# Products of zeros ahead of the first scores, and squares in pieces of two heads

## The chip, the cores and the metric

One core of a Trainium2 chip runs the kernel. The metric is the device time of one execution in microseconds; the kernel before took 604.68 us (median of 3 runs, 604.56 to 605.29). The core has four engines that matter here: TensorE (PE: matrix products; its weight loads are a row of their own, PEld), VectorE (DVE), ScalarE (ACT) and GpSimd (POOL). SP issues transfers. Each engine takes its instructions strictly from its own queue, in the order in which the program was built; semaphores hold an instruction until what it needs is there.

## The reference

Cosine attention over 8 batches, 12 heads, 448 tokens, 64 columns a head, and then a mixer with a low-rank product over the tokens and a two-layer network (MLP):

```python
q_n = q / (norm(q) + 1e-6);  k_n = k / (norm(k) + 1e-6)
attn = softmax(q_n @ k_n.T / tau)
x = (attn @ v)                       # heads side by side: 448 x 768
u = x + ((x.T @ U) @ V).T            # U: 448 x 32, V: 32 x 448
out = u + relu(u @ w_ch1) @ w_ch2    # 768 -> 3072 -> 768
```

## The kernel before

The work goes batch by batch. **Statistics**: q and k of four heads come in one transfer each (`load_qk`; batch 0's first two heads by SP, the next two by POOL). `squares` squares them on ScalarE or VectorE (L456, L458) and sums each head's 64 columns on VectorE (L462); `scales` makes from this the inverse norm (ScalarE's logarithm and exponential L475, L478, VectorE L481, L483), and `norm` multiplies (L537, tile `xn`, "unit buffer"). A pair of heads is then transposed into `qkT`: for batches 0 and 1 by TensorE (`flip`, L374) with copies out of its bank by ScalarE or VectorE (L827, L829), later by a transposing transfer. **Attention**: for each pair, seven score products of 128x448 (L573), seven exponentials on ScalarE (L578), 32 products with the values (L595, into the ring `av` of two banks), and a reciprocal and a scaling on VectorE (L602, L604) into `X_sb`. **Low rank**: `stage0` makes A = U'X (L652) and then u = X + V'A: products (L631 and L733 in batch 0, L687 after it) and VectorE's sums (L696, L698, L701). **MLP**: up products with w1 (L763), the rectifier on ScalarE or VectorE (L786, L788), down products with w2 (L797), sums into `O_sb` (L806) and out.

The PSUM banks are split into three rings: `mm` (3 banks: transposes, up and down products and others), `sc` (3: scores, and batch 1's low-rank products) and `av` (2).

The order on each engine is written by a planner that is part of the kernel. Every operation is an `Op` with an engine, a guessed duration, what it depends on, and the ring slots that it takes and frees. `Plan.run` plays them in time; an engine that is free takes the first operation that is ready. TensorE's operations stand in streams, tried in the order in which the streams were made: transposes, batch 0's scores, value products, low rank, other scores, MLP. What the planner writes is the order of the instructions; its times are not used for anything else. So an edit of a guessed duration, or one more operation, can move instructions anywhere in the program. For the first pair of batch 0 the guesses are larger than elsewhere: 0.09 for a transpose, 0.31 for a score product, 0.09 for a value product, against 0.05, about 0.19 and 0.033 later.

In this program the ring of squares (`sq`) has two buffers for four heads each.

Of the kernel before, what the change touches and what calls it, by code (L numbers as in the profile page):

```python
# [11 lines left out]
BF = mybir.dt.bfloat16  # L12
# [192 lines left out]
def kernel(  # L205
# [12 lines left out]
    nc = tc.nc  # L218
# [13 lines left out]
    EPS = 1e-6  # L232
    PE_BATCHES = 2
    LATE, VLATE = 8.0, 3.2

    const = ctx.enter_context(tc.tile_pool(name="const", bufs=1))
    pool = ctx.enter_context(tc.tile_pool(name="pool", bufs=1))
# [9 lines left out]
    def ring(n, shape, dt, name, space=None):  # L247
        p = space or pool
        return Ring(n, lambda i: p.tile(shape, dt, name=name, tag=name, bufs=n))
# [7 lines left out]
    v_t = fixed(2, [128, H, 4, D + 2], BF, "v_nat")  # L257

    r_ld, r_xn, r_attn = fixed_ring(ld_t), fixed_ring(xn_t), fixed_ring(attn_t)
    r_sq = ring(2, [SCH, G, SC * D], BF, "sq")  # L260
    r_ss = ring(4, [SCH, 2, G, SC], FP, "ss")
    r_ln = ring(4, [SCH, 2, G, SC], FP, "ln")
    r_inv = ring(4, [SCH, 2, G, SC], FP, "inv")
# [34 lines left out]
    U_sb = const.tile([128, 2, 4, R], BF, name="U_sb")  # L298
    V_sb = const.tile([128, PAD + S + PAD], BF, name="V_sb")
    ident = const.tile([128, 128], BF, name="ident")  # L300
    w1_sb = const.tile([128, CC, F], BF, name="w1_sb")

    nc.scalar.preload_act_table_set("natural_log_exp_and_others")
# [17 lines left out]
    pe_a = plan.stream("PE")  # L321
    pe_sc = plan.stream("PE")
    pe_mlp = plan.stream("PE")
    pool_q = plan.stream("POOL")

    def pe_t(n):
# [115 lines left out]
    def squares(b, g, ld, ops, lo, ii, ss, pr, on, hold, then):  # L442

        red = []
        for i in ii:
            for a0 in range(0, g, G):
                a1 = min(g, a0 + G)
                sq = Slot(r_sq, 1)
                n = 256 * (a1 - a0)
                o = Op(on, {"ACT": act_t(n), "DVE": dve_t(n, 1.45)} if "/" in on else act_t(n) if on == "ACT" else dve_t(n, 1.45), None,  # L450
                       deps=[ops[i], *hold], acq=[sq], prio=pr + 0.2, fast=True)

                def square(o=o, i=i, a0=a0, a1=a1, sq=sq):
                    x, y = ld.tile[:, i, lo + a0:lo + a1, :], sq.tile[:, 0:a1 - a0, :]
                    if o.by == "ACT":
                        nc.scalar.activation(out=y, in_=x, func=AF.Square)  # L456
                    else:
                        nc.vector.tensor_mul(y, x, x)  # L458
                o.fn = square
                plan.add(o)  # L460
                red.append(plan.add(Op("DVE", dve_t(256 * (a1 - a0)),
                    lambda i=i, a0=a0, a1=a1, sq=sq: nc.vector.reduce_sum(  # L462
                        ss.tile[:, i, a0:a1, :].rearrange("p h c -> p (h c)"),
                        sq.tile[:, 0:a1 - a0, :].rearrange("p h (c d) -> p (h c) d", d=D),
                        axis=AX.X),
                    deps=[o, *then], acq=[ss], rel=[sq], prio=pr + 0.1)))
        return red
# [49 lines left out]
    def norm(b, p, ld, la, inv, a, deps, pr):  # L517


        by_pe = b < PE_BATCHES  # L520
        first = b == 0 and p == 0
        xn, qkT = Slot(r_xn, 3 if first else 2 if by_pe else 1), Slot(r_qkT, 7)
        need = [xn_set[count[0] % len(xn_t)]]
        count[0] += 1

        def part(i, h0=0, h1=2):
            def fn():
                n = h1 - h0
                src = ld.tile[:, i, la + h0:la + h1, :].rearrange("p h (c d) -> p h c d", d=D)
                sc = inv.tile[:, i, a + h0:a + h1, :].unsqueeze(3).to_broadcast([SCH, n, SC, D])  # L530
                if i == 0:
                    dst = xn.tile[:, 8:12, :].rearrange("p c (h d) -> p h c d", h=2)
                else:
                    dst = xn.tile.rearrange("p b e -> p (b e)")[:, 0:9 * 128].rearrange(
                        "p (h x) -> p h x", h=2)[:, h0:h1, 0:SC * 128].rearrange(
                        "p h (c e) -> p h c e", c=SC)[:, :, :, 0:D]
                nc.vector.tensor_mul(dst, src, sc)  # L537
            return plan.add(Op("DVE", dve_t(256 * (h1 - h0)), fn, deps=need + [deps[i]], acq=[xn],
                               rel=[getattr(ld, "slot", ld), inv], prio=pr))

        if first:
            ops = [part(0), part(1, 0, 1), part(1, 1, 2)]
            blocks = [(8, 12, ops[0]), (0, 4, ops[1]), (4, 8, ops[2])]
        else:
            ops = [part(1), part(0)]
            blocks = [(0, 8, ops[0]), (8, 12, ops[1])]
        if not by_pe:
            done = [plan.add(Op("SP", 0.1, lambda: nc.sync.dma_start_transpose(
                out=qkT.tile, in_=xn.tile.rearrange("p b e -> p (b e)")), deps=ops, acq=[qkT],
                rel=[xn], prio=0, lat=("x", 0.05 * 84, LATE)))]  # L550
        else:
            done = []
            for b0, b1, o in blocks:
                done.append(flip(
                    pe_tp, [(lambda z=z: xn.tile[:, z, :]) for z in range(b0, b1)], SCH,
                    lambda: qkT.tile, (lambda t_, x, b0=b0, b1=b1: key_tiles(t_, x, b0 // 4, b1 // 4)
                                   if b == 0 and b0 < 8 else [(t_[:, b0:b1, :], x)]),
                    [o], [qkT], [xn], 1, "ACT/DVE", 0.09 if first else 0.05, b == 0 and b0 < 8))
        got[b, p, "qkT"] = (qkT, lambda m: (done[:2] if m < 3 else done) if first else done, done)
        return ops  # L560


    def attention(b, p, X):
        off = PAD * (b % 2)
        qkT, qdeps, _ = got.pop((b, p, "qkT"))
        attn = Slot(r_attn, 2)
        exps = {}
        for m in (0, 1, 2, 6, 3, 4, 5) if b == 0 else range(7):
            sc = Slot(r_sc, 1)

            def score(sc=sc, m=m):
                kT = qkT.tile[:, 0:8, :].rearrange("p b s -> p (b s)")
                nc.tensor.matmul(out=sc.tile[:, 0:S], lhsT=kT[:, 128 * m:128 * (m + 1)],  # L573
                                 rhs=qkT.tile[:, 8:12, :].rearrange("p c s -> p (c s)"),
                                 start=True, stop=True)
            o = plan.add(Op("PE", 0.31 if b == 0 and p == 0 else pe_t(S), score, deps=qdeps(m), acq=[sc], rel=[qkT]),
                         pe_first if b == 0 else pe_sc)
            exps[m] = plan.add(Op("ACT", act_t(S), lambda sc=sc, m=m: nc.scalar.activation(  # L578
                out=attn.tile[:, m, off:off + S], in_=sc.tile[:, 0:S], func=AF.Exp,
                scale=inv_tau), deps=[o], acq=[attn], rel=[sc], prio=0.1 if b == 0 else 1))  # L580
        last_exp[b] = exps[5]
        if b == 0 and p == 0:
            last_exp["first"] = [exps[1]]
        muls = []
        for hh in range(2):
            h = 2 * p + hh
            av, rd = Slot(r_av, 1), Slot(r_rd, 1)
            mine = [3 * hh, 3 * hh + 1, 3 * hh + 2, 6] if b == 0 else [4 * hh, 4 * hh + 1, 4 * hh + 2, 3]
            need = [exps[m] for m in mine]
            for t in range(4):  # L590
                for j in range(4):
                    first, last = t == 0 and j == 0, t == 3 and j == 3
                    def fn(t=t, j=j, h=h, mine=mine, av=av):
                        m = mine[j]
                        nc.tensor.matmul(  # L595
                            out=av.tile[:, t, 0:D + 1],
                            lhsT=attn.tile[:, m, 128 * t:128 * (t + 1)],
                            rhs=v_t[b % 2][:, h, j, 0:D + 1], start=(j == 0), stop=(j == 3))
                    o = plan.add(Op("PE", 0.09 if b == 0 and p == 0 else 0.033, fn,
                        deps=need + got[b, h, "v"] + attn_set + [v_set[b % 2]] if first else (), acq=[av] if first else [],  # L600
                        rel=[attn] if last else []), pe_av)
            r = plan.add(Op("DVE", 0.20, lambda av=av, rd=rd: nc.vector.reciprocal(  # L602
                out=rd.tile, in_=av.tile[:, :, D:D + 1]), deps=[o], acq=[rd], prio=1))
            muls.append(plan.add(Op("DVE", dve_t(256), lambda av=av, rd=rd, h=h: nc.vector.tensor_mul(  # L604
                X.tile[:, :, h * D:(h + 1) * D], av.tile[:, :, 0:D],
                rd.tile.to_broadcast([128, 4, D])), deps=[r],
                acq=[X], rel=[av, rd], prio=1)))
        last_av[b, p] = o
        return muls
# [258 lines left out]
                       in_=V_f().rearrange("r (s c) -> r c s", c=SC))  # L868


    w2_ops = []
    NW = 4
    THIRDS = [(0, 4), (4, 8), (8, 12)]
# [109 lines left out]
```

## Time and profile before

| | |
|---|---|
| median of 3 runs | 604.68 us |
| profiled execution, its own time | 604.68 us |
| its span, first to last instruction | 602.8 us |
| busy: TensorE, weight loads | 586.0 us (97%), 347.7 us |
| busy: VectorE, ScalarE, GpSimd | 295.9, 277.9, 116.3 us |
| mean granted TensorE clock | 0.997 |
| first matmul | at 7.24 us |
| first up product of batch 1 | at 111.14 us |

A line of the timeline gives the start and the length in us, the engine, the source line, the operation, the tile written and the tiles read, the shapes and how many were merged. A line of the groups gives the sum of the busy time and the mean duration in ns. The chain of waits is followed back from the last instruction; each piece says what the end of the program hung on at that time. Matmuls are pipelined: the length of a single one includes its way through the array, and a run of n of them gives their pace. Other groups that the text uses:

```profile
L374 PE MATMUL tp<-ident,xn 112*128 112x112 bf16 x144 | 12.0, 234 | 9.2 <-DVE xn L537 9.1
L604 DVE TENSOR_TENSOR X_sb<-av,rd 128x256 bf16<-128x256 f32 x96 | 40.3, 421 | 1.8
L701 DVE TENSOR_TENSOR u_nat<-mm,X_sb 128x384 bf16<-128x384 f32 x36 | 19.1, 552 | 15.5 <-PE mm L687 15.4
```

### The profile page before, as it was taken

The page shows a single profiled execution, that of the slowest core. Times are in us where ns is not written, and L with a number is a line of the kernel's source. Part 1 is how long each engine was busy: PE and PEld are TensorE (multiplying, and loading weights), DVE is VectorE, ACT ScalarE, POOL GpSimd, SP SyncE. Part 2 cuts the span into 40 slices and gives each one's busy share as a digit, 9 for nine tenths or more (in the row PEclk, how much of TensorE's full clock was granted, in tenths as well). Part 3 has the DMA queues.
Part 4 walks back from the last instruction along what each step waited for, and adds up shares of the span by engine and source line. Part 5 has one row for each costly group of instructions (what it writes and reads, how often), then busy time and mean ns, then how long its engine had stood idle before and what let it go on. Part 6 is the DMA issues. An engine that isn't in the chain of part 4 may idle for free.

```text
span 602.8 us, 11404 instructions
## 1 busy us (share of the span) xinstructions
PE 586.0 (97%) x4702; PEld 347.7 (58%) x4725; DVE 295.9 (49%) x630; ACT 277.9 (46%) x601; POOL 116.3 (19%) x178
## 2 busy tenths in 40 slices
PE   4899999999999999999999999999999999999997
PEld 2566666555565665666445666566545666654565
DVE  8968749989997998554721244014300210110011
ACT  7777762477775277316741067505642025014300
POOL 8155434153613516000600000000000000000000
PEclk9899999999999999999999999999999999999999
DMA  9999999999998989715932132030002110310021
GB/s 147 187 162 119 200 204 119 142 161 112 153 166 138 187 128 150 104 53 93 123 26 66 53 74 47 1 93 27 15 1 53 52 40 1 89 43 1 0 54 53
DMA packets 150164, 54.81 MB, mean 91 GB/s; under 512 B 115040, under 2 KB 150112, under 8 KB 150112
## 3 DMA queue, kind: packets, MB, share of 16 engines
q0 software_dynamic: 72864, 25.73, 38.4%
q1 hardware_dynamic: 77184, 28.32, 25.1%
q8 instruction: 37, 0.61, 0.4%
q14 instruction: 15, 0.12, 0.1%
q10 hardware_dynamic: 64, 0.02, 0.0%
HBM read 52.25 MB, written 11.01 MB: 105 GB/s over the span
## 4 chain that ended last, share of the span: by engine, by line
PE 89%; DVE 7%; ACT 2%; issue 1%; DMA 1%
PE mm L763 35%; PE mm L797 32%; PE sc L573 10%; PE av L595 7%; DVE ss L462 2%; DVE xn L537 2%; PE tp L374 1%; PE mm L687 1%; ACT attn L578 1%; DVE sq L458 1%; DVE u_nat L701 1%; PE mm L652 1%; DVE O_sb L806 1%; PE sc L763 1%; DMA raw_uv<-in_q_dram 1%
## 5 line engine op out<-in xcount | busy, mean ns | idle before, releaser
L763 PE MATMUL mm<-uT,w_sb 128*128 128x384 bf16 (+1 forms) x1112 | 236.4, 353 | 1.5 <-DVE relu L788 0.4
L797 PE MATMUL mm<-w_sb,relu 128*128 128x384 bf16 (+1 forms) x1368 | 233.8, 324 | 0.1
L578 ACT ACTIVATE attn<-sc 128x448 bf16<-128x448 f32 x336 | 165.1, 552 | 111.1 <-PE av L595 56.4
L797 PEld LDWEIGHTS <-relu 128*128 128x128 bf16 x1368 | 132.5, 98 | 85.9 <-issue 0.4
L763 PEld LDWEIGHTS <-w_sb 128*128 128x128 bf16 x1152 | 112.1, 98 | 103.5 <-issue 1.5
L786 ACT ACTIVATE relu<-mm 128x512 bf16<-128x512 f32 (+1 forms) x157 | 85.8, 547 | 130.6 <-PE mm L763 130.1
L806 DVE TENSOR_TENSOR O_sb<-mm,u_nat 128x384 f32<-128x384 f32 (+1 forms) x57 | 31.1, 549 | 213.5 <-PE mm L797 210.0
L573 PE MATMUL sc<-qkT 128*128 128x448 bf16 x336 | 106.6, 364 | 1.8 <-ACT qkT L827 0.6
L595 PEld LDWEIGHTS <-attn 128*128 128x128 bf16 x1536 | 62.5, 99 | 18.2 <-issue 3.0
L418 POOL DMA_DIRECT2D v_nat<-in_v_dram x98 | 63.1, 652 | 32.0 <-DMA w_sb<-in_moe_w_ch_dram 13.1
L595 PE MATMUL av<-v_nat,attn 128*128 128x65 bf16 x1536 | 66.4, 195 | 0.3 <-DVE X_sb L604 0.3
L537 DVE TENSOR_TENSOR xn<-qk_nat,inv 112x512 bf16<-112x512 bf16 x94 | 61.8, 687 | 2.7 <-DMA qkT<-xn 2.6
L462 DVE TENSOR_REDUCE ss<-sq 112x16 f32<-112x1024 bf16 (+1 forms) x50 | 58.0, 1166 | 0.8 <-ACT sq L456 0.4
L396 POOL DMA_DIRECT2D qk_nat<-in_q_dram x24 | 17.2, 717 | 133.8 <-DVE xn L537 100.4
L573 PEld LDWEIGHTS <-qkT 128*128 128x128 bf16 x336 | 29.6, 99 | 20.6 <-issue 5.7
L604 DVE TENSOR_TENSOR X_sb<-av,rd 128x256 bf16<-128x256 f32 x96 | 40.3, 421 | 1.8
L602 DVE RECIPROCAL rd<-av 128x4 f32<-128x4 f32 x96 | 17.1, 179 | 38.6 <-PE av L595 37.9
L458 DVE TENSOR_TENSOR sq<-qk_nat 112x1024 bf16<-112x1024 bf16 x45 | 29.8, 671 | 0.0
L788 DVE TENSOR_SCALAR relu<-mm 128x384 bf16<-128x384 f32 (+1 forms) x32 | 19.7, 615 | 14.6 <-PE mm L763 13.8
L701 DVE TENSOR_TENSOR u_nat<-mm,X_sb 128x384 bf16<-128x384 f32 x36 | 19.1, 552 | 15.5 <-PE mm L687 15.4
L374 PE MATMUL tp<-ident,xn 112*128 112x112 bf16 x144 | 12.0, 234 | 9.2 <-DVE xn L537 9.1
L475 ACT ACTIVATE ln<-ss 112x32 f32<-112x32 f32 (+2 forms) x26 | 6.0, 230 | 28.6 <-DVE ss L462 28.6
(60 smaller groups left out, 169.4 us busy)
## 6 DMA issues: line engine op xcount, KB each, us to landing
qk_nat<-in_q_dram POOLq DMA_DIRECT2D x23, 224.0 KB, 5.4
qk_nat<-in_k_dram POOLq DMA_DIRECT2D x23, 224.0 KB, 6.2
w_sb<-in_moe_w_ch_dram POOLq DMA_DIRECT2D x4, 1152.0 KB, 13.6
w_sb<-in_moe_w_ch_dram POOLq DMA_DIRECT2D x8, 576.0 KB, 15.7
out_dram<-O_sb SPq DMA_DIRECT2D x15, 168.0 KB, 2.3
out_dram<-O_sb SPq DMA_DIRECT2D x16, 144.0 KB, 2.1
out_dram<-O_sb SPq DMA_DIRECT2D x16, 120.0 KB, 2.0
out_dram<-O_sb SPq DMA_DIRECT2D x16, 96.0 KB, 2.2
```

Source lines behind the costliest of these rows:

```text
L418: nc.gpsimd.dma_start(out=vb[p0:p0 + s1 - s0, hs, j, 0:D], in_=v[b, hs].rearrange("h (s c) d -> c s h d", c=SC)[c, s0:s1]),
L458: nc.vector.tensor_mul(y, x, x)
L462: lambda i=i, a0=a0, a1=a1, sq=sq: nc.vector.reduce_sum(ss.tile[:, i, a0:a1, :].rearrange("p h c -> p (h c)"), sq.tile[:, 0:a1 - a0, :].re ...
L537: nc.vector.tensor_mul(dst, src, sc)
L573: nc.tensor.matmul(out=sc.tile[:, 0:S], lhsT=kT[:, 128 * m:128 * (m + 1)], rhs=qkT.tile[:, 8:12, :].rearrange("p c s -> p (c s)"), start=T ...
L578: exps[m] = plan.add(Op("ACT", act_t(S), lambda sc=sc, m=m: nc.scalar.activation(out=attn.tile[:, m, off:off + S], in_=sc.tile[:, 0:S], fu ...
L595: nc.tensor.matmul(out=av.tile[:, t, 0:D + 1], lhsT=attn.tile[:, m, 128 * t:128 * (t + 1)], rhs=v_t[b % 2][:, h, j, 0:D + 1], start=(j == ...
L604: muls.append(plan.add(Op("DVE", dve_t(256), lambda av=av, rd=rd, h=h: nc.vector.tensor_mul(X.tile[:, :, h * D:(h + 1) * D], av.tile[:, :, ...
L763: o = plan.add(Op("PE", pe_t(n), lambda cc=cc: nc.tensor.matmul(out=mm.tile[:, 0:n], lhsT=w1_sb[:, cc, f * 128:(f + 1) * 128], rhs=uT.tile ...
L786: nc.scalar.activation(out=relu.tile[:, f, 0:n], in_=mm.tile[:, 0:n], func=AF.Relu)
L797: nc.tensor.matmul(out=mm.tile[:, 0:c1 - c0], lhsT=relu.tile[:, f, i * 128:(i + 1) * 128], rhs=w2_t[:, f, c0:c1], start=(f == 0), stop=(f ...
L806: nc.vector.tensor_add(out=O.tile[:, 0:w], in0=mm.tile[:, 0:w], in1=us[i].tile[:, c0:c1]),
```

## The change

Three things are edited. A tile of zeros is set by VectorE, and TensorE gets 52 products of it (128x208) in a stream of its own, the last to be tried, so that the planner puts them where nothing else is ready; all write one bank of the ring `av`, which is free again after the last of them. The squares and their sums are cut into pieces of two heads in all batches, with new guesses of their duration, and the two buffers hold two heads. The larger guesses for the first pair's transposes, scores and value products are replaced by those of the other pairs. Fills of U, V and the third unit buffer by POOL, and batch 1's fill of v, are the same in both kernels.

```diff
+    WARM = 52
-    r_sq = ring(2, [SCH, G, SC * D], BF, "sq")
+    r_sq = ring(2, [SCH, G // 2, SC * D], BF, "sq")
+    warm = const.tile([128, 208], BF, name="warm")
+    pe_warm = plan.stream("PE")
...
-            for a0 in range(0, g, G):
-                a1 = min(g, a0 + G)
+            for a0 in range(0, g, G // 2):
+                a1 = min(g, a0 + G // 2)
                 sq = Slot(r_sq, 1)
-                n = 256 * (a1 - a0)
-                o = Op(on, {"ACT": act_t(n), "DVE": dve_t(n, 1.45)} if "/" in on else act_t(n) if on == "ACT" else dve_t(n, 1.45), None,
+                o = Op(on, 0.48 if on == "ACT" else 0.44, None,
                        deps=[ops[i], *hold], acq=[sq], prio=pr + 0.2, fast=True)
...
-                    [o], [qkT], [xn], 1, "ACT/DVE", 0.09 if first else 0.05, b == 0 and b0 < 8))
+                    [o], [qkT], [xn], 1, "ACT/DVE", 0.05, b == 0 and b0 < 8))
...
-            o = plan.add(Op("PE", 0.31 if b == 0 and p == 0 else pe_t(S), score, deps=qdeps(m), acq=[sc], rel=[qkT]),
+            o = plan.add(Op("PE", pe_t(S), score, deps=qdeps(m), acq=[sc], rel=[qkT]),
...
-                    o = plan.add(Op("PE", 0.09 if b == 0 and p == 0 else 0.033, fn,
+                    o = plan.add(Op("PE", 0.033, fn,
...
+    warm_set = fill(lambda: nc.vector.memset(warm, 0.0), 60, prio=-9)
+    hot = Slot(r_av, WARM)
+    for _ in range(WARM):
+        plan.add(Op("PE", 0.18, lambda: nc.tensor.matmul(
+            out=hot.tile.rearrange("p t d -> p (t d)")[:, 0:208], lhsT=warm[:, 0:128], rhs=warm,
+            start=True, stop=True), deps=[warm_set], acq=[hot], rel=[hot]), pe_warm)
```

The built programs differ in the order of their queues from the start on. What of this the prediction uses: the place of the zero products (36 ahead of the first transpose, then 3, 6, 6 and 1 up to the first pair's last scores), the products of batch 0's MLP that stand ahead of batch 1's first transposes and around its low-rank products, and VectorE's order there.

## The prediction

> **What bounds the kernel now.** I read the page, then TensorE's work in ten-microsecond windows, then the timeline and the chain of waits at the two places that the edit reaches. The profiled execution took 604.68 us, a span of 602.8 and 1.9 around it; it is also the median (runs 604.56 to 605.29), so sums against it are sums against the median.
>
> The windows, columns PE, PEld, DVE, ACT, POOL busy (instructions), granted clock, DMA share, GB/s:
>
> ```profile
> 0.00:10.00 10.00, 2.44 (x15) 1.42 (x16) 7.42 (x23) 5.94 (x17) 8.85 (x18) 1.00 1.17 143
> 10.00:20.00 10.00, 7.77 (x56) 4.38 (x54) 9.59 (x17) 8.36 (x21) 5.18 (x8) 1.00 1.45 158
> 20.00:30.00 10.00, 9.12 (x114) 6.41 (x115) 9.68 (x27) 7.98 (x21) 2.10 (x3) 0.83 1.12 202
> 50.00:60.00 10.00, 10.00 (x79) 6.32 (x78) 8.63 (x15) 8.60 (x21) 7.77 (x12) 1.00 1.09 78
> 100.00:110.00 10.00, 10.00 (x74) 6.05 (x72) 9.79 (x21) 2.22 (x7) 1.41 (x2) 1.00 0.60 103
> ```
>
> From about 30 us on TensorE is full; before that it is short of work while VectorE is full. So the time is TensorE's work plus its idle time: what starts it sooner is a gain, and any later hole in its queue is a loss, one for one.
>
> The early matmuls ran at half clock. Three single score products of one shape:
>
> ```profile
> 16.04 0.56 PE L573 MATMUL sc<-qkT 128*128 128x448 bf16 x1
> 24.49 0.56 PE L573 MATMUL sc<-qkT 128*128 128x448 bf16 x1
> 29.43 0.35 PE L573 MATMUL sc<-qkT 128*128 128x448 bf16 x1
> ```
>
> and the granted clock in half-microsecond windows:
>
> ```profile
> 18.00:18.50 0.50, 0.50 (x13) 1.00 1.23 220
> 19.00:19.50 0.50, 0.00 (x0) 1.00 1.21 209
> 22.50:23.00 0.50, 0.50 (x4) 0.50 1.28 230
> 26.00:26.50 0.50, 0.50 (x10) 1.00 1.31 208
> ```
>
> The product at 16.04 took what the one at a recorded 0.50 took (0.56), so the 1.00 there is not to be believed; full speed (0.35) held for good from 25.5 us. The recorded half clock, about 22.2 to 25.5, follows a stretch with 1.6 us idle and then two dozen transposes.
>
> **Zero products.** 52 matmuls of 128x208 are added, 36 queued ahead of the first transpose, 3, 6, 6 and 1 between the first pair's steps. No row has 208 columns; three scores at half clock pace at 1.12/3 = 0.373 us for 448 columns, at full clock 0.19, so 208 columns are 0.173 or 0.088 (bounds: the 112-column transposes' 0.095, the 448-column 0.373). The memset of their tile waits for nothing (VectorE starts at 0.92) and costs about 0.14 by the rows of 36 and 256 elements (0.09, 0.27); VectorE's 0.43 idle before 4.54 hides it, else it would delay the first norm by 0.14. The 36 end at latest at 1.1 + 36 x 0.173 = 7.3; the first transpose starts at 7.24 now. Cost 0 to 0.1. The bank that they hold is free at about 10.6, before the first value product (15.2).
>
> If they warm the clock, how much is on the path? The chain:
>
> ```profile
> 8.45 1.22 ACT qkT L827 x6
> 13.54 1.51 DVE ss L462 x2
> 19.58 1.89 DVE xn L537 x3
> 30.44 3.17 ACT attn L578 x7
> ```
>
> It runs over ScalarE's copies and VectorE's statistics up to 19.6. Faster transposes bring the key copies forward 0.2, and the query copy (0.56) now goes ahead of them on ScalarE. From 20.3 to 25.6 TensorE is on the chain, cold from 22.2: 3.4 us of work, 1.7 to be saved if the clock stays up. But the clock fell at 22.2 after just such a gap, and the zeros are all used by about 11, so I count half of the 1.7. [...]
>
> **Squares in pieces of two heads.** Two rows become four, all along the kernel:
>
> ```profile
> L462 DVE TENSOR_REDUCE ss<-sq 112x16 f32<-112x1024 bf16 x46 | 55.3, 1209 | 0.4
> L458 DVE TENSOR_TENSOR sq<-qk_nat 112x1024 bf16<-112x1024 bf16 x45 | 29.8, 671 | 0.0
> L462 DVE TENSOR_REDUCE ss<-sq 112x8 f32<-112x512 bf16 x4 | 2.6, 682 | 0.4 <-ACT sq L456 0.4
> ```
>
> A half reduction is 0.64 to 0.68, so each pair costs 0.1 more than the whole. VectorE has no half square; between 0.30 (half the chain's 0.60) and 0.60, I take 0.35. That is 46 x 0.2 = 9 us of VectorE over the kernel, hidden under the MLP's products while these are at hand; price uncovered 0 to 2.
>
> Until the third pair's first norm (12.02 to 19.58 now, 7.56), VectorE's new queue holds 5 half squares, 6 half reductions, one copy of 0.38 and about 0.5 of small steps: 1.75 + 3.84 + 0.38 + 0.5 = 6.5, plus about 0.6 waiting for ScalarE's second half square, which stands behind a pair of copies and an exponential: 7.1. Gain 0.45; the other two reductions come after and push the fifth pair's norms back about 1 us, which fourteen exponentials cover. With 0.2 from the copies and half of 1.7: about 1.0 to 1.5. ScalarE limits from there (18 exponentials without a break to 38.2) and gets 0.5 to 1 more work. I take **-1.0**; bounds -2.4 (0.7 + 1.7) and +0.3.
>
> **The moved order.** The removed guesses of slow products change the order that the kernel's planner writes, and this I weigh most. The built queue has 125 of batch 0's 144 up products ahead of batch 1's first transposes, against 47. So batch 1's attention ends late against batch 0's MLP, which is the only filler. How its end is covered now:
>
> ```profile
> 89.61 0.68 DVE L696 TENSOR_TENSOR u_nat<-sc,X_sb 64x512 bf16<-64x512 f32 x1
> 90.31 0.69 DVE L698 TENSOR_TENSOR u_nat<-sc,X_sb 64x512 bf16<-64x512 f32 x1
> 90.66 1.62 PE L797 MATMUL mm<-w_sb,relu 128*128 128x384 bf16 x9
> 98.00 0.68 PE L595 MATMUL av<-v_nat,attn 128*128 128x65 bf16 x16
> 106.59 4.71 PE L797 MATMUL mm<-w_sb,relu 128*128 128x384 bf16 x28
> 111.14 1.03 PE L763 MATMUL mm<-uT,w_sb 128*128 128x512 bf16 x3
> ```
>
> First place: the low-rank products for columns 0 to 640 share three banks, freed by VectorE's sums. Between the first and last of them stand 30 down products (4.9 us) now, one afterwards. TensorE then waits for VectorE's queue: result 0.6, sums 1.37, 1.29, a scaling 0.42, sums 0.60 and 0.48, a hop 0.1 = 4.9; its own work in it is 5 x 0.216 + 5 x 0.056 + 0.163 = 1.5. Hole: **3.4**.
>
> Second place: after the last value products 66 down products (10.8 us) stand before batch 1's first up product now, 10 afterwards. VectorE's new queue there: reciprocal and scaling 0.8, inverse 0.34, half reduction 0.64, an output sum 0.55, four norms 2.40, two sums 0.48, half square 0.35, sum 0.29, half reduction 0.64, two sums 0.40 = 6.9. TensorE's work: 10 x 0.163, four scores 0.76, six transposes 0.34, low-rank 0.5 = 3.2. Hole: **3.7**.
>
> In the trace these stretches lose little: 8.74 busy of 9.00 from 88 to 97, 14.92 of 15.00 to 112, so 0.4. Net 3.4 + 3.7 - 0.4 = +6.7; I take **+6.5**. Bounds: +4 (half squares at 0.30, the first hole's scores already drained in part) and +9 (VectorE, 98% busy, late by another 1 to 2). If the holes shut the clock as the gap before 22.2 did, 3.4 us at half speed cost 1.7 more. The second weights' last piece landed at 86.3; the new order asks for it at about 86 (what is queued ahead of it from 43.1 on, at the warm paces of the trace), cost 0 to 1.
>
> Sum: 604.7 - 1.0 + 6.5 = **610.2**; with the bounds 606 to 615.
>
> **Rivals.**
> *The start alone counts*: -1.0 to -2.4, 602.3 to 603.7. For it: the early clock is plainly half. Against: the queues are in order, and VectorE's list after the last value products is unconditional. Needs the holes to be under 1 us. Chance 0.13.
> *Both cancel*: the start at its best and holes of 2 to 3: about 604.7. Chance 0.09.
> *The zeros come late or don't warm*: if each also pays its weight load (0.10 by the page's PEld rows), 36 x 0.273 = 9.8, the first transpose slips 3.7 and, with the holes, the time is about 614 (610.2 + 3.7). The score pace of 0.373, which is the bare column time, speaks against. It decides as soon as the 36 end after 7.3. If they merely don't warm, the gain is gone: 611. Chance 0.08.
> *The forecast*: holes larger than the gain, 606 to 614: chance 0.70.
>
> **How the numbers follow.** This kernel's measurement tells 0.2% (1.2 us) from no change. Faster 0.13; same 0.09; slower 0.70 + 0.08 = 0.78. The likeliest case's own range is 606 to 614; reaching to part of the cancelling case, 604 to 614 leaves out the faster case and a few in a hundred above.
>
> **What would show it.** Right: scores of 0.35 before 15 us; first up product 0.5 to 1.5 sooner than 41.6; then, between about 98 and 112, windows in which TensorE is idle 3 us and more beside a full VectorE, with the chain going over the sums into u and the norms. Wrong: no such idle time; or the first transposes well after 7.3; or TensorE stalled on the second weights at 80 to 87; or early scores still at 0.56.

## The result, and the profile after

The changed kernel takes **614.09 us** (median of 4 runs, 612.95 to 616.24) against 604.62 (604.25 to 605.29) beside it: ratio 1.016, 95% interval 1.0125 to 1.0194. The direction and the places were forecast; the time lies just above the range's end of 614.0. The profiled execution took 613.0 us, a span of 611.2. All ratios below are against the kernel before, run beside.

Windows of the changed kernel, columns as before (busy of PE, PEld, DVE, ACT, POOL with counts, granted clock, DMA share, GB/s):

```profile
0.00:10.00 10.00, 7.66 (x66) 6.34 (x67) 7.52 (x25) 6.87 (x20) 8.84 (x18) 1.00 1.14 142
10.00:20.00 10.00, 6.28 (x73) 3.66 (x73) 9.59 (x21) 9.22 (x25) 5.15 (x8) 1.00 1.52 165
20.00:30.00 10.00, 9.25 (x116) 5.89 (x114) 9.51 (x26) 9.21 (x25) 2.50 (x5) 0.83 1.10 198
100.00:110.00 10.00, 7.17 (x58) 4.43 (x58) 9.91 (x23) 2.50 (x5) 1.68 (x3) 0.83 1.13 132
...
103.00:106.00 3.00, 0.94 (x5) 0.36 (x5) 2.97 (x6) 0.00 (x0) 1.04 (x2) 1.00 0.96 135
106.00:109.60 3.60, 3.32 (x23) 2.42 (x23) 3.56 (x11) 1.45 (x2) 0.00 (x0) 0.54 1.48 171
...
115.00:118.00 3.00, 0.46 (x3) 0.11 (x2) 2.92 (x8) 0.67 (x2) 1.00 (x2) 1.00 0.64 143
...
121.00:124.00 3.00, 3.00 (x20) 1.47 (x18) 2.18 (x9) 1.56 (x4) 0.00 (x0) 0.61 1.41 152
```

From 100 to 110 TensorE was full before, with 74 products; now it does 58. The two holes are plain: 0.94 and 0.46 us of work in 3 us, beside a full VectorE. Behind each stands a stretch at half clock: 0.54 and 0.61 in windows that are nearly full (3.32 of 3.60 and 3.00 of 3.00).

The timeline of TensorE shows the early scores at full speed (0.35, where the kernel before had 0.56 at 16.04), then what it waits for:

```profile
10.10 0.35 PE L575 MATMUL sc<-qkT 128*128 128x448 bf16 x1
15.09 0.35 PE L575 MATMUL sc<-qkT 128*128 128x448 bf16 x1
...
103.69 0.39 PE L689 MATMUL sc<-A_sb,V_sb 128*128 128x512 bf16 x1 [1.13 <-DVE u_nat L700]
105.94 0.22 PE L689 MATMUL sc<-A_sb,V_sb 128*128 128x128 bf16 x1 [0.71 <-DVE u_nat L703]
108.92 2.65 PE L799 MATMUL mm<-w_sb,relu 128*128 128x384 bf16 x13
117.26 0.23 PE L689 MATMUL sc<-A_sb,V_sb 128*128 128x128 bf16 x1 [1.32 <-DVE u_nat L700]
```

The brackets give the idle time and who ended it: VectorE's sums into u, which free the three banks, as forecast. And the chain of waits goes over VectorE's norms and sums:

```profile
99.87 1.80 DVE xn L539 x3
...
102.94 0.69 DVE u_nat L700
...
103.67 1.29 DVE u_nat L703 x2
...
114.30 2.40 DVE xn L539 x4
116.70 0.19 DVE u_nat L698
116.91 0.29 DVE u_nat L700
```

This sign alone says little, for in the kernel before the chain went over the same groups here:

```profile
103.36 0.60 DVE xn L537
...
104.49 0.36 DVE u_nat L701 x2
...
104.90 1.28 DVE xn L537 x2
```

There TensorE had down products to do meanwhile; it is the empty windows that set the two apart.

The costliest groups of the halves (sum of busy time, mean ns):

```profile
L464 DVE TENSOR_REDUCE ss<-sq 112x8 f32<-112x512 bf16 x96 | 63.6, 675 | 0.8 <-ACT sq L458 0.5
L460 DVE TENSOR_TENSOR sq<-qk_nat 112x512 bf16<-112x512 bf16 x89 | 34.5, 413 | 1.8 <-DMA qk_nat<-in_q_dram 1.8
```

For sums below I use one more reading of the trace, called **stall**: for each matmul, the time from the end of the one before to its own end, less what it takes at full clock: 2.5 ns and its columns at 2.4 a ns, the pace of this trace (163 ns for 384 columns, 189 for 448, 216 for 512), and 32 ns for the products of 65 columns. Half clock shows up in it as well as idling. A few matmuls are missing from most profiles (23 before, 26 changed); each counts as stall, at most 0.6 us in the row from 100 to 130.

| us | before | changed |
|---|---|---|
| first up product starts at | 39.63 | 37.76 |
| stall from 40 to 100 us | 1.1 | 0.5 |
| stall from 100 to 130 us | 1.0 | 11.6 |
| stall from 130 to 200 us | 1.05 | 1.2 |

Changed minus before: -1.9 - 0.6 + 10.6 + 0.15 = +8.3, about the difference of the spans (8.4). Of the 11.6, two granted stretches of half clock (106.26 to 109.67 and 119.91 to 123.33), at most 1.7 each, are up to 3.4.

### The profile page after: what moved, and what is told of

Same layout as the page of the kernel before. It is cut to its first block, busy times and chain, and to the rows that moved or that the text cites. A ratio compares the mean times of both kernels' runs of the same rounds, so it can differ in the third digit from the quotient of the medians.

```text
span 611.2 us, 11622 instructions
## 1 busy us (share of the span) xinstructions
PE 592.5 (97%) x4751; PEld 352.8 (58%) x4777; DVE 300.7 (49%) x717; ACT 280.1 (46%) x607; POOL 116.0 (19%) x178
## 4 chain that ended last, share of the span: by engine, by line
PE 77%; DMA 12%; DVE 4%; POOL 3%; issue 2%; SPq 1%; ACT 0%; POOLq 0%
PE mm L765 31%; PE mm L799 30%; PE sc L575 8%; DMA w_sb<-in_moe_w_ch_dram 6%; PE av L597 6%; DMA v_nat<-in_v_dram 3%; DMA qk_nat<-in_q_dram 1%; POOL qk_nat L399 1%; DVE xn L539 1%; PE mm L689 1%; POOL v_nat L421 1%; DMA raw_uv<-in_moe_V_dram 1%; DMA raw_uv<-in_moe_U_dram 1%; POOL w_sb L362 1%; DVE ss L464 1%
## 5 line engine op out<-in xcount | busy, mean ns | idle before, releaser
L788 ACT ACTIVATE relu<-mm 128x512 bf16<-128x512 f32 (+1 forms) x164 | 89.5, 545 | 134.9 <-PE mm L765 134.2
L575 PE MATMUL sc<-qkT 128*128 128x448 bf16 x336 | 102.7, 358 | 3.5 <-ACT qkT L829 1.3
L597 PEld LDWEIGHTS <-attn 128*128 128x128 bf16 x1536 | 62.3, 98 | 18.5 <-issue 3.6
L464 DVE TENSOR_REDUCE ss<-sq 112x8 f32<-112x512 bf16 x96 | 63.6, 675 | 0.8 <-ACT sq L458 0.5
L460 DVE TENSOR_TENSOR sq<-qk_nat 112x512 bf16<-112x512 bf16 x89 | 34.5, 413 | 1.8 <-DMA qk_nat<-in_q_dram 1.8
L790 DVE TENSOR_SCALAR relu<-mm 128x384 bf16<-128x384 f32 (+1 forms) x25 | 15.5, 622 | 12.1 <-PE mm L765 11.7
L399 POOL DMA_DIRECT2D qk_nat<-in_k_dram x24 | 16.9, 705 | 5.8 <-DMA w_sb<-in_moe_w_ch_dram 5.7
```

The source lines that it names most:

```text
L399: ops = [load(lambda i=i, src=src: nc.gpsimd.dma_start(out=ld.tile[:, i, lo:lo + h1 - h0, :], in_=src[b, h0:h1].rearrange("h (s c) d -> s ...
L464: lambda i=i, a0=a0, a1=a1, sq=sq: nc.vector.reduce_sum(ss.tile[:, i, a0:a1, :].rearrange("p h c -> p (h c)"), sq.tile[:, 0:a1 - a0, :].re ...
L597: nc.tensor.matmul(out=av.tile[:, t, 0:D + 1], lhsT=attn.tile[:, m, 128 * t:128 * (t + 1)], rhs=v_t[b % 2][:, h, j, 0:D + 1], start=(j == ...
L788: nc.scalar.activation(out=relu.tile[:, f, 0:n], in_=mm.tile[:, 0:n], func=AF.Relu)
```

## The experiments

**What moved the order?** The prediction laid it to the removed guesses of slow products. The halves and the guesses can each be built alone (the zeros come with the guesses in e2, below); the counts of the order tell them apart already, and the chip confirms it.

e3, the halves alone (beside the ring of two heads):

```diff
-            for a0 in range(0, g, G):
-                a1 = min(g, a0 + G)
+            for a0 in range(0, g, G // 2):
+                a1 = min(g, a0 + G // 2)
...
-                o = Op(on, {"ACT": act_t(n), "DVE": dve_t(n, 1.45)} if "/" in on else act_t(n) if on == "ACT" else dve_t(n, 1.45), None,
+                o = Op(on, 0.48 if on == "ACT" else 0.44, None,
```

> The kernel before with the squares in pieces of two heads and their flat guesses 0.48 and 0.44; no zero products, the first pair's products guessed as before. Its order has 125 up products ahead of batch 1's transposes and 1 and 10 down products at the two places, as the changed kernel has. Theory 'order moved by the halves' guesses': the two holes and 1.7 of half clock behind each are there, about +10.6 from 100 to 130 us, and 614 to 616 us with a small early gain or none. Rival, as the prediction put it ('the removed guesses of slow products change the order'): without removing them no holes, 604 to 605.

Measured: 614.54 us (613.77 to 614.78), ratio 1.015, 1.0136 to 1.0164. Stall from 100 to 130 us: 11.6, as in the changed kernel.

e4, the guesses alone:

```diff
-                    [o], [qkT], [xn], 1, "ACT/DVE", 0.09 if first else 0.05, b == 0 and b0 < 8))
+                    [o], [qkT], [xn], 1, "ACT/DVE", 0.05, b == 0 and b0 < 8))
...
-            o = plan.add(Op("PE", 0.31 if b == 0 and p == 0 else pe_t(S), score, deps=qdeps(m), acq=[sc], rel=[qkT]),
+            o = plan.add(Op("PE", pe_t(S), score, deps=qdeps(m), acq=[sc], rel=[qkT]),
```

(and the value products' 0.09 likewise)

> The kernel before with only the first pair's guesses replaced (0.05, 0.19 and 0.033 for transposes, scores and value products). Its order from batch 1's transposes on is that of the kernel before (47, 30, 66). Theory 'order moved by the halves' guesses': 604 to 605, no holes. Rival, as the prediction put it: the holes come with these guesses, 610 or more.

Measured: 604.74 (604.33 to 605.54), ratio 0.9994, 0.9985 to 1.0003; stall from 100 to 130 us 1.0. So the halves, with their guesses, carry the holes, and the prediction's cause falls.

**Is it the halves' work or only their guess?** e1 is the changed kernel, operation for operation, with another guess (with the order, some copies and rectifiers change places between ScalarE and VectorE):

```diff
-                o = Op(on, 0.48 if on == "ACT" else 0.44, None,
+                o = Op(on, {"ACT": act_t(256 * (a1 - a0)), "DVE": dve_t(256 * (a1 - a0), 1.45)} if "/" in on else act_t(256 * (a1 - a0)) if on == "ACT" else dve_t(256 * (a1 - a0), 1.45), None,
```

> The changed kernel with one thing edited: the planner's guess for a square of two heads is worked out per element as before (0.480 us on ScalarE, 0.436 on VectorE) in place of the flat 0.48 and 0.44. Every instruction is the same; the order differs: 66 of batch 0's 144 up products stand ahead of batch 1's first transposes (125 in the changed kernel), 27 down products between batch 1's low-rank products (1), 69 after its last value products (10). Theory 'order': the holes at 101 to 121 us and the two stretches of half clock behind them go, the early gain of about 1.9 stays: 602 to 604 us. Rival 'halves': it is VectorE's nine microseconds more that TensorE waits for, wherever its products stand: 610 or more.

Measured: 604.61 (603.82 to 606.96), ratio 0.999, 0.9979 to 1.0. Its windows at the two places:

```profile
103.00:106.00 3.00, 3.00 (x29) 1.93 (x26) 2.96 (x8) 0.85 (x2) 0.00 (x0) 1.00 0.26 71
...
115.00:118.00 3.00, 3.00 (x16) 1.42 (x15) 3.00 (x8) 2.34 (x7) 0.57 (x1) 1.00 0.71 157
```

VectorE is as full as in the changed kernel (2.96 and 3.00 of 3), and TensorE has work: 29 and 16 products for 5 and 3. So VectorE's additional work is not what is waited for; what stands beside its queue is. (That work is also less than the prediction's 9 us: busy 300.7 us against 295.9.) Of other guesses I have only the orders that the planner writes: a flat 0.436 in place of 0.44 already has e1's counts (66, 27, 69), 0.45 has those of 0.44 (125, 1, 10). By the counts, four nanoseconds of a guess decide about nine microseconds of the time.

**The banks.** e7 leaves the halves' guess and mends what starved: the planner lets batch 1's transposes wait 0.8 us after a bank comes free, the up products 0.25, so that up products can take bank after bank ahead of them. In e7 the transposes wait 0.3.

```diff
                             rel=rel if z == len(ins) - 1 else []), stream)
+            o.safe = min(o.safe, 0.3)
```

> The changed kernel with one more line in the planner's input: the safety time that batch 1's transposes have to wait after a bank is freed is 0.3 us in place of 0.8, near the 0.25 of the up products that compete for the same banks. The early order is the changed kernel's; 54 up products stand ahead of batch 1's transposes, 27 and 69 down products at the two places. Theory 'starved transposes': no holes, no half clock behind 30 us, and the changed kernel's early part: 603 to 604.5 us, 0.5 to 2 less than before. Rival 'VectorE is too full with halves in all batches': waits for norms turn up elsewhere between 50 and 130 us, 605 to 608.

Measured: 605.1 (603.71 to 607.44), ratio 1.0005, 0.9994 to 1.0016. The holes are gone (stall 1.3 from 100 to 130 us), so the transposes' safety time is where the order tips. But nothing is gained over the kernel before: the stall from 40 to 100 us is 2.5 against 1.1. Of it, four transposes of batch 1 account for 0.8 us at 50 to 60 and 0.3 at 70 to 80 us, one of them released by a norm of VectorE, the others by copies and rectifiers. So the rival's waits are there, but small, and only in part for norms.

**The clock behind the holes.** e5 keeps the changed kernel's order and puts 76 zero products into the holes after planning (40 and 36):

```diff
+    ZEROS = ({962: 2, 964: 12, 965: 4, 966: 4, 967: 3, 968: 4, 969: 7, 970: 4},
+             {1040: 2, 1041: 7, 1042: 13, 1043: 5, 1044: 6, 1051: 3})
...
+                for _ in range(places.get(n_pe, 0)):
...
+                    nc.tensor.matmul(out=bank[hole].rearrange("p t d -> p (t d)")[:, 0:208],
+                                     lhsT=warm[:, 0:128], rhs=warm, start=True, stop=True)
```

> The changed kernel with 76 more zero products (128x208) written into its order after planning: 40 between batch 1's low-rank products (101 to 107 us) and 36 in the second hole (114 to 121 us), placed by the stalls there, 0.089 us each, 3.6 and 3.2 us in all, a little less than the stalls. Nothing else moves. Theory 'clock': the holes stay as long as they are, but the two stretches of 3.41 us at half clock behind them go, 1.7 us each: 3.0 to 3.4 us less than the changed kernel, 610 to 611.5 us. Rival 'the holes are all of it' (VectorE is late after them too, so full clock gains nothing): 613 to 614.5. Rival 'zeros delay': 615 or more.

Measured: 611.23 (609.59 to 613.49), ratio 1.0103, 1.0086 to 1.0121: three to four microseconds under the changed kernel by work that computes nothing. Windows of e5:

```profile
106.00:109.00 3.00, 3.00 (x34) 2.76 (x33) 2.96 (x6) 0.00 (x0) 1.41 (x2) 1.00 1.22 105
109.00:112.00 3.00, 3.00 (x37) 2.42 (x35) 2.96 (x9) 1.08 (x2) 0.00 (x0) 1.00 1.35 186
...
118.00:121.00 3.00, 2.50 (x26) 2.01 (x25) 2.92 (x8) 0.17 (x1) 1.41 (x2) 1.00 0.70 142
121.00:124.00 3.00, 2.85 (x34) 1.95 (x33) 3.00 (x9) 2.21 (x7) 0.00 (x0) 1.00 1.41 86
```

The clock stays at 1.00. What is left, about 6 us over the kernel before, is in the main the idle time itself, which the zeros now fill.

**How many stretches of half clock?** e6 is the changed kernel without its zero products, e13 the changed kernel itself once more.

```diff
-    warm_set = fill(lambda: nc.vector.memset(warm, 0.0), 60, prio=-9)
-    hot = Slot(r_av, WARM)
-    for _ in range(WARM):
...
```

> The changed kernel without the zero products and their tile; squares in halves and the new guesses stay, and so does the order from batch 1's transposes on (125, 1, 10). Theory 'zeros don't count' (VectorE's statistics and ScalarE's exponentials set the early part, and half the clock there costs nothing): first up product within 0.5 of the changed kernel's 37.8 or of 38.8 (halves alone), 613.5 to 615 us. Rival 'warm clock', the prediction's 0.2 + 0.85 for it: 1 us later and 615 to 616.

> The changed kernel once more, for its second profile. Theory 'the windows of the clock are free-running': the stretches of half clock behind the two holes start at other times and last 3.41 or 6.83 us each, so that runs spread over 612.5 to 617 us. Theory 'the early gain of 1.9 in the first profile was half luck' (its third pair's k landed at 9.2 us, the zero-product runs' at 10.1 to 10.9): with k landing near 10.7 the first up product comes at 38.6 to 39.1; with k at 9.3 at 37.8. Rival 'the early gain is the change's own 1.9': 37.8 whenever k lands.

e6: 616.38 (613.2 to 617.45), ratio 1.018, 1.0159 to 1.0202. e13: 615.57 (612.7 to 617.1), ratio 1.016, 1.014 to 1.018. Windows of e6 cut at the clock's own steps:

```profile
104.40:107.81 3.41, 1.41 (x7) 0.45 (x6) 3.37 (x7) 0.00 (x0) 1.41 (x2) 1.00 0.76 118
107.81:111.23 3.42, 2.68 (x20) 2.10 (x20) 3.38 (x11) 0.92 (x1) 0.00 (x0) 0.50 1.35 160
111.23:114.64 3.41, 3.41 (x12) 1.65 (x11) 2.48 (x5) 1.10 (x4) 0.00 (x0) 0.50 0.65 115
114.64:118.05 3.41, 3.41 (x40) 2.12 (x39) 2.10 (x7) 0.46 (x2) 0.00 (x0) 1.00 0.02 5
```

Here the hole spans parts of two windows, and both that follow are at half clock: 6.8 us behind each hole (107.81 to 114.64 and 121.47 to 128.29), four stretches of 3.41 in all. The first profile had two, e13's three:

```profile
109.42:112.83 3.41, 3.41 (x17) 1.84 (x15) 3.41 (x10) 1.85 (x4) 0.00 (x0) 0.50 1.14 175
...
119.66:123.07 3.41, 2.23 (x10) 1.09 (x9) 3.38 (x10) 1.41 (x3) 0.92 (x2) 0.50 0.99 129
123.07:126.48 3.41, 3.41 (x24) 1.79 (x22) 2.40 (x8) 1.95 (x7) 0.00 (x0) 0.50 1.36 156
```

Stalls from 100 to 130 us: 11.6, 12.3 and 13.9 with two, three and four stretches. A stretch costs 1.7 us if TensorE has work all through it, less otherwise: by the columns streamed in them (448 columns pace at 373 ns in the half clock of the first profile and of the one before, at 189 in the full) the stretches added about 3.1, 4.5 and 5.7 us. That leaves 8.5, 7.8 and 8.2 us of idling. So the idle part is nearly the same, and the clock's part goes with the number of stretches. The nine runs of the changed kernel agree: the mean granted clock is 0.992 to 0.994 in those of 612.7 to 614.7 us, and 0.986 to 0.989 in those of 615.2 to 617.1.

The early part differs too. e13's first up product came at 38.40, with the third load's k landed at 10.11 (9.23 in the first profile); e6's at 39.47, with k at 11.22. That the first profile's early gain of 1.9 was in part a transfer that landed early fits these three but isn't shown: in e7, whose early order is the changed kernel's, k landed at 10.38 and the first up product still came at 37.74. e7's windows from 15.44 to 25.68 are all at 1.00, where the first profile has half clock from 20.93 to 24.34.

**The early part.** e2: zero products and new guesses, squares whole as before.

```diff
-    warm = const.tile([128, 208], BF, name="warm")
+    warm = const.tile([128, 128], BF, name="warm")
...
-            out=hot.tile.rearrange("p t d -> p (t d)")[:, 0:208], lhsT=warm[:, 0:128], rhs=warm,
+            out=hot.tile.rearrange("p t d -> p (t d)")[:, 0:208], lhsT=warm, rhs=warm[:, 0:104].unsqueeze(1).to_broadcast([128, 2, 104]),
```

> Zero products and the new guesses for the first pair, squares and sums in whole pieces of four heads as before (the tile of zeros is 128 wide and read twice over, for room). 42 up products ahead of batch 1's transposes, 35 and 65 down products at the two places. Theory 'order': no holes there, and the zeros' share of the early gain: first up product between 38.5 and 39.4 (before 39.6, changed 37.8), 603.3 to 604.4 us. Rival 'the early gain is all the zeros': first up product at 37.8, 602.5 to 603. Rival 'zeros cost': 604.6 or more.

Measured: 604.58 (603.38 to 605.34), ratio 0.9991, 0.9982 to 0.9999; first up product at 39.75, no sooner than before (39.63), though with k at 10.75 against 9.35. e8 is the changed kernel with halves in batch 0 alone:

```diff
-            for a0 in range(0, g, G // 2):
-                a1 = min(g, a0 + G // 2)
+            for a0 in range(0, g, G if b else G // 2):
+                a1 = min(g, a0 + (G if b else G // 2))
...
```

> Zero products and new guesses as in the changed kernel, but halves only in batch 0 (where the first statistics are waited for) and whole squares behind it; the two buffers hold four heads again, the tile of zeros is 128 wide. Its order: 65 up products ahead of batch 1's transposes, 30 and 72 down products at the two places. Theory: early gain of the halves (0.8 or more) without VectorE's nine microseconds more: 603 to 604.3 us. Rival 'nothing of the early gain is left at the end': 604.6 to 605.5.

Measured: 604.35 (603.04 to 606.2), ratio 0.9986, 0.9976 to 0.9996. Then the same without the 52 zeros (e10: the block with `warm` taken out), with 25 more that hold the clock from 17 us on (e9, below), and with those 25 alone, at the same places (e12; the cut is e9's):

```diff
+    ZEROS = {122: 18, 130: 2, 134: 3, 142: 2}
...
+                nc.tensor.matmul(out=nxt.tile[:, 0:208], lhsT=warm, rhs=warm[:, 0:104].unsqueeze(1).to_broadcast([128, 2, 104]),
+                                 start=True, stop=True)
```

> The kernel of e8 without its zero products: halves in batch 0 alone and the new guesses; same order from batch 1's transposes on. Theory 'zeros don't count': 604.1 to 604.8 us, as e8's 604.35. Rival 'the zeros bring the early gain': 605 or more.

> The kernel of e8 (zero products, halves in batch 0 alone) with 25 more zero products before and between the two groups of transposes that follow the idle stretch at about 17 us: 18 ahead of the third pair's first transpose (1.6 us in a stall of 1.9), then 2, 3 and 2 at stalls of 0.2 to 0.45. They write the bank of the next score product. The half clock that every profile but one so far shows between 16 and 27 us should go. Theory 'the early clock is worth time' (the prediction's 1.7 us): first up product near 38, 603 to 603.7 us. Rival 'ScalarE and VectorE set the early part': clock at 1.00 throughout and first up product as in e8 or 0.3 sooner, 604 to 604.6.

> The kernel of e10 (halves in batch 0 alone, none of the change's 52 zero products) with only the 25 zero products of e9, from the idle stretch at about 17 us on. Theory 'zeros are worth time only where the clock would shut': as e9 or better, 602.8 to 603.6 us, no half clock behind 17 us in the profile. Rival 'clock worth nothing': as e10, 603.7. Rival 'the 52 early ones carry e9': 604 or more.

| | median us | ratio, 95% interval | recorded half clock from 13.3 to 28 us | first up product |
|---|---|---|---|---|
| e8: 52 zeros | 604.35 | 0.9986, 0.9976 to 0.9996 | 20.1 to 26.9 | 39.13 |
| e9: 52 + 25 | 603.59 | 0.998, 0.9971 to 0.9989 | none | 37.77 |
| e10: none | 603.69 | 0.9981, 0.9973 to 0.999 | 20.1 to 23.5 | 38.85 |
| e12: 25 | 604.04 | 0.9987, 0.9979 to 0.9996 | none | 38.29 |

The clock's record of e10 begins at 13.3 us, with its step to full speed. Windows of e10 and of e9 over the same stretch:

```profile
18.00:22.00 4.00, 2.27 (x25) 1.88 (x26) 4.00 (x9) 2.14 (x6) 0.00 (x0) 0.77 1.16 195
22.00:26.00 4.00, 3.81 (x47) 2.25 (x46) 3.93 (x12) 4.00 (x12) 0.50 (x2) 0.81 1.20 233
```

```profile
18.00:22.00 4.00, 3.42 (x44) 2.53 (x42) 4.00 (x10) 2.21 (x7) 0.00 (x0) 1.00 1.14 191
22.00:26.00 4.00, 3.20 (x49) 2.10 (x47) 3.93 (x12) 3.94 (x12) 0.29 (x1) 1.00 1.18 228
```

The held clock is seen, and in single profiles the first up product comes 0.6 to 1.4 sooner with it; but VectorE (4.00, then 3.93 of 4) and, from 22 us, ScalarE (4.00 and 3.94) are as full either way, and the times don't follow: all four intervals overlap, and e10, with no zero at all, is as good as e9. That zeros this early are worth time is not shown. e9 and e10 are 0.2% faster than the kernel before.

**The price of halves on VectorE.** e11 keeps the order before and writes each square on VectorE and each sum as two instructions in place.

```diff
-                        nc.vector.tensor_mul(y, x, x)
+                        for c0 in range(0, a1 - a0, 2):
+                            nc.vector.tensor_mul(y[:, c0:c0 + 2, :], x[:, c0:c0 + 2, :], x[:, c0:c0 + 2, :])
...
```

> The kernel before, its order kept exactly, with each square on VectorE and each sum written as two instructions of two heads in the place of the one of four: what the pieces cost VectorE without any move. Half sums and half squares cost it about 0.12 us a sum and 0.08 us a square more (675 against 1209 ns, 413 against 671 by the profiles' means), some 9 us over the kernel. Theory, as the prediction put it: hidden under the MLP's products, 604.6 to 605.5. Rival: TensorE waits for it, 606 to 610.

Measured: 605.81 (605.37 to 607.14), ratio 1.0017, 1.0008 to 1.0026: 0.5 to 1.6 us come through. In its profile VectorE's busy time rose by 3.1 us, from 295.9 to 299.0. Part of the loss lies at the start (first up product at 40.60), where k landed late as well (10.90 against 9.35).

## Why the prediction was right and where it failed

**The holes: right.** Place, cause and size hold. Forecast 3.4 + 3.7 - 0.4 = 6.7, taken as 6.5; the idle part measured is 7.8 to 8.5 less the 1.0 that was there before: 6.8 to 7.5.

**The clock behind them: the step that failed.** "If the holes shut the clock as the gap before 22.2 did, 3.4 us at half speed cost 1.7 more" stood beside the sum, which counts it at nothing, and speaks of one stretch. It happened behind each hole, for one or two stretches: about 3.1 us in the first profile, 4.5 and 5.7 in e13 and e6, and e5, which keeps the clock up, is three to four faster. With two stretches at the prediction's own 1.7 the forecast would have been 610.2 + 3.4 = 613.6. The profile before had it too: the gap ahead of 20 us, with 1.6 us idle, was shorter than either forecast hole, and half clock stands behind it from 22.13 to 25.54. Here the price of a hole was its length and the half clock after it. The first profile hides part of it: its 1.9 us at the start, for the 1.0 forecast, and 0.6 less stall from 40 to 100 us took back 1.5 of what the clock cost.

**The cause of the order: wrong.** "The removed guesses of slow products change the order" is refuted by e4; the halves' flat guess does it (e3, e1), through the 0.8 us that batch 1's transposes must wait for a bank (e7). The counts of the order were right, so the sum was not touched by it; but who had put the old guesses back would have mended nothing (e3 has them: 614.54).

**The early gain: about right in sum, open in its parts.** Forecast were 0.45 from the halves, 0.2 from the key copies and 0.85 from the clock, 1.5 in all, taken as 1.0 for ScalarE's sake. The first profile had 1.9, the second 1.2 (39.63 to 38.40), e1's times 0 to 1.3. What the half clock costs there stays open. e4's profile has it over two windows (19.1 to 25.9), and its first up product stands at 39.72 against 39.63; against that stand e7's 37.74 and the 0.6 to 1.4 of e9 and e12, all in single profiles, while the times show no difference clear of noise. Of the statistics in halves the times show more: e10, without any zero, is 1.2 faster (0.6 to 1.6), where the guesses alone (e4) gain nothing clear.

**Zeros that come at no cost: right.** The 36 ended at 5.77, before 7.3; early scores took 0.35. That the gap at 17 to 18.5 would shut the clock again was the other half of the 1.7, and half clock did come, from 20.93 to 24.34 (0.83 in the window 20 to 30).

**VectorE's halves: hidden, mostly, and cheaper than 9 us.** 413 ns a square for the 350 taken, 675 a sum as taken from its row. But lengths of records don't add up to VectorE's time: it was busy 4.8 us longer in the changed kernel (300.7 against 295.9) and 3.1 in e11. Priced uncovered 0 to 2, e11 has 0.5 to 1.6.

**The second weights: a little more than 0 to 1.** TensorE idles 0.3 us for them in the first profile and 1.5 in e13 (ahead of the down products at 83.5 and 85.4). Such a stall was among the prediction's signs of being wrong; it came beside the holes, not in their place:

```profile
L799 PE MATMUL mm<-w_sb,relu 128*128 128x384 bf16 x1320 | 229.5, 327 | 1.5 <-DMA w_sb<-in_moe_w_ch_dram 1.5
```

In e5's profile it is 2.3, in that of the kernel before there is none: the new order asks for them as they land.

**The rivals.** "The start alone counts" needed holes under 1 us; "both cancel" holes of 2 to 3. The first transposes came at 7.07, so the zeros were not late, and they sped up as they ran, from 173 ns each for the first 16 to 89 from 3.9 us on; the scores behind them took 0.35, those of the kernel before 0.56. So they warm.

## What to carry to other kernels

Where a planner writes the order, read the queues that come out before pricing an edit's instructions, and build each part of the edit alone to see which one moves them: here a guess, of which no instruction knows, outweighed all else in the change. Price a hole in TensorE's queue with the half clock behind it: here one or two stretches of 3.41 us behind each hole, up to 1.7 us apiece. A warm clock was worth three to four microseconds behind the holes, where TensorE had work waiting (e5); ahead of 28 us, beside full VectorE and ScalarE rows, no gain clear of noise was shown for it.

## What the runs showed of the hardware

**The granted clock as recorded.** In the profile before, half clock is recorded from 22.13 to 25.54 us; in the first profile of the changed kernel from 20.93 to 24.34, 106.26 to 109.67 and 119.91 to 123.33. Each of these stretches lasts 3.41 us, and the full clock between them 81.92 and 10.24, 24 and 3 times as long. In e13 the stretches behind the holes stand elsewhere, from 109.42 to 112.83 and 119.66 to 126.48. TensorE's busy time in windows of that length, cut at these steps: at the holes, half clock followed windows at full clock with 0.96 to 1.76 us (0.96 and 1.41 in e6, 1.09 and 1.48 in the first profile, 1.28 and 1.76 in e13), and in the profile before one with 1.52 (18.72 to 22.13). Around 2 us it went either way: full clock followed 1.98 in e7 (15.44 to 18.86) and 2.04, twice, in the first profile (10.69 to 14.10 and 113.08 to 116.50), half clock 1.99 in e5 (12.21 to 15.62) and 2.06 in the first profile (17.51 to 20.93). What the clock goes by is not shown.

**Windows with transposes.** In e7, the window from 18.86 holds 24 transposes and three other products:

```profile
18.86:22.27 3.41, 2.53 (x27) 1.58 (x28) 3.41 (x7) 2.46 (x8) 0.00 (x0) 1.00 1.20 206
22.27:25.68 3.41, 2.68 (x43) 1.84 (x43) 3.34 (x11) 3.35 (x10) 0.29 (x1) 1.00 1.19 238
```

and in e5, the window from 12.21 twenty products and no transpose:

```profile
12.21:15.62 3.41, 1.99 (x20) 0.99 (x20) 3.01 (x6) 3.41 (x10) 3.06 (x5) 1.00 1.47 120
15.62:19.04 3.42, 2.34 (x22) 1.33 (x19) 2.44 (x7) 3.23 (x9) 1.71 (x3) 0.50 1.17 142
```

The clock stayed behind the first and fell behind the second. In the changed kernel's first profile, the window from 17.51 holds 24 transposes and two other products, and the clock fell behind it (2.06 us busy, half clock from 20.93). Whether transposes differ from other products in this is not shown.

**A load's landing.** The third load's k in batch 0, issued at 3.42 to 3.44 us in every profile, landed between 9.2 and 11.2 us, in the changed kernel alone at 9.23 and 10.11. What an early gain of one microsecond is worth can't be read from single profiles.
